# Three parameter loads moved to GpSimd's queue, the weights of gate tiles 0 to 3 issued back to back on SyncE, the parameter transpose moved behind quarter 1, x of block 2 loaded in four parts

## The chip, the cores and the metric

The kernel runs on one core of a Trainium2 chip. Times are device microseconds (us) of one execution; lower is better. A "span" is the time from the first to the last instruction in a trace; the device time of the same execution is 1.7 to 1.9 us longer, and 2.2 to 2.4 us longer in 7 of the 109 executions that have both numbers. A ratio is the mean time of one kernel's runs over that of the other's runs of the same rounds, so it is not quite the ratio of the medians quoted beside it.

Engines: PE is TensorE (matmul), PEld its weight loads, DVE is VectorE, ACT is ScalarE, POOL is GpSimd, SP is SyncE. A name with q, such as SPq, is the engine's instruction stream where it issues DMAs.

## The reference

A layernorm feeds two branches, an S5 state-space scan and a gated MLP, and all is summed. S is 2048, D is 512, F is 1792.

```python
xn = layernorm(x)
# branch A: diagonal complex recurrence
dt = exp(log_dt);  Lam_bar = exp(dt * (Lambda_re + 1j * Lambda_im))
h_t = Lam_bar * h_(t-1) + B_bar @ xn_t
y   = 2 * real(C @ h) + xn * Dskip
# branch B: gated MLP
out_B = (silu(xn @ w1) * (xn @ w3)) @ w2
return x + y + out_B
```

The parameters of this document are the three vectors log_dt, Lambda_re and Lambda_im, 512 bf16 numbers (1 KB) each. They are loaded as 12 rows of 128, transposed on PE, and turned into the table of angles for the scan.

## The kernel before

The start of the kernel issues loads by hand. Everything that SyncE issues goes out in program order:

```python
    def load_w(f0, f1, eng1=nc.sync, eng3=nc.sync):                    # w1: gate side, w3: up side
        eng1.dma_start(out=w1_sb[:, :, f0:f1], in_=w1v[:, :, f0:f1])   # line 151
        eng3.dma_start(out=w3_sb[:, :, f0:f1], in_=w3v[:, :, f0:f1])   # line 152
    ...
    for c in range(2):                                                  # x chunks 0 and 1 in halves
        for eng, dsl in ((nc.sync, slice(0, D // 2)), (nc.scalar, slice(D // 2, D))):
            eng.dma_start(out=x_blk[0][:, c, dsl], in_=xv[:, c, dsl])
    nc.scalar.dma_start(out=x_blk[0][:, 3, :], in_=xv[:, 3, :])
    nc.sync.dma_start(out=x_blk[0][:, 2, :], in_=xv[:, 2, :])
    load_w(0, 2 * P)                                                    # tiles 0 and 1
    for i, src in enumerate((A_log_dt, A_Lambda_re, A_Lambda_im)):      # line 166 is the DMA
        nc.sync.dma_start(out=par_rows[i * NPT:(i + 1) * NPT, :], in_=src.rearrange("(t p) -> t p", p=P))
    load_w(2 * P, 4 * P)                                                # tiles 2 and 3
```

The first block of 512 rows is treated in four quarters of 128 rows, as the x chunks arrive. A quarter's matmuls (line 557) need that chunk normalised and transposed (line 238), and the weights of its tiles. Tiles 0 and 1 write gu_ps, tile 2 writes bu_ps:

```python
            quarter(0, (0, 1), 2)          # needs w1, w3 of tiles 0 and 1
            pps = params_transpose()       # needs par_rows; line 310
            params_dt(pps)
            params_turn()                  # a row of small GpSimd instructions
            table_angles(0)                # VectorE, four instructions each
            table_angles(1)
            quarter(1, (0, 1))
            ln_first_transpose(2)
            quarter(0, (2,))               # needs w1, w3 of tile 2
            ln_first_transpose(3)
            quarter(1, (2,))
            ...                            # [cut: quarters 2 and 3, then 512-column matmuls, line 525]
```

The later loads, issued on SyncE at about 33 us, contain:

```python
        load_x(2)                          # x of block 2, one DMA of 512 KB
        load_x(3)
```

Of the kernel before, what the change touches and what calls it, by code (L numbers as in the profile page):

```python
# [17 lines left out]
P = 128  # L18
# [45 lines left out]
def kernel(  # L64
# [17 lines left out]
    nc = tc.nc  # L82
# [8 lines left out]
    NPT = PS // P  # L91
# [41 lines left out]
    par_rows = const.tile([3 * NPT, P], BF16, name="par_rows")  # L133
# [16 lines left out]
    def load_w(f0, f1, eng1=nc.sync, eng3=nc.sync):  # L150
        eng1.dma_start(out=w1_sb[:, :, f0:f1], in_=w1v[:, :, f0:f1])  # L151
        eng3.dma_start(out=w3_sb[:, :, f0:f1], in_=w3v[:, :, f0:f1])  # L152

    def load_x(b, parts=1):
        n = CPB // parts
        for i in range(0, CPB, n):
            nc.sync.dma_start(out=x_blk[b][:, i:i + n, :], in_=xv[:, b * CPB + i:b * CPB + i + n, :])
# [4 lines left out]
    nc.scalar.dma_start(out=x_blk[0][:, 3, :], in_=xv[:, 3, :])  # L162
    nc.sync.dma_start(out=x_blk[0][:, 2, :], in_=xv[:, 2, :])
    load_w(0, 2 * P)
    for i, src in enumerate((A_log_dt, A_Lambda_re, A_Lambda_im)):
        nc.sync.dma_start(out=par_rows[i * NPT:(i + 1) * NPT, :], in_=src.rearrange("(t p) -> t p", p=P))  # L166
    load_w(2 * P, 4 * P)

    def bulk_loads():
        nc.scalar.activation(out=w1_sb[:, 0, 4 * P:4 * P + 1], in_=rstd_all[:, 0:1], func=ACT.Copy)  # L170
        load_w(4 * P, MID * P)
        load_x(1)
        nc.sync.dma_start_transpose(out=bt[:, 0], in_=A_B_re)
        nc.sync.dma_start_transpose(out=bt[:, 1], in_=A_B_im)
        load_w(MID * P, F)
        nc.sync.dma_start_transpose(out=ct_in[:, :, 0, :], in_=A_C_re)
        nc.sync.dma_start_transpose(out=ct_in[:, :, 1, :], in_=A_C_im)

    def late_loads():
        nc.sync.dma_start(out=w2_sb, in_=B_w2.rearrange("(t p) d -> p t d", p=P))  # L180
        nc.sync.dma_start(out=dskip_row, in_=A_Dskip.partition_broadcast(P))
        load_x(2)
        load_x(3)


# [5 lines left out]
    def keep_busy(n, cols):  # L191
        for _ in range(n):
            nc.tensor.matmul(out=wps[:, 0:cols], lhsT=ones[:, 0:P], rhs=ones[:, 0:cols], start=True, stop=True)
# [4 lines left out]
    nc.gpsimd.memset(ident, 0.0)  # L198
    nc.gpsimd.affine_select(out=ident, in_=ident, compare_op=ALU.not_equal, fill=1.0,
                            base=0, pattern=[[-1, P]], channel_multiplier=1)  # L200
    nc.gpsimd.iota(iota_i, pattern=[[1, TBLK]], base=1, channel_multiplier=0)
    nc.gpsimd.tensor_copy(out=iota_f, in_=iota_i)
    nc.gpsimd.memset(halfpi, float(np.pi / 2))
# [8 lines left out]
    def ln_stats(b, cl):  # L212
        stats = lnp.tile([P, 6], FP32, name="stats", bufs=4)
        nc.vector.bn_stats(out=stats, in_=x_blk[b][:, cl, :])
        nc.vector.bn_aggr(out=mv_all[:, b * CPB + cl, :], in_=stats)
# [10 lines left out]
    def ln_first_rstd(cl):  # L226
        lnv = lnp.tile([P, 1], FP32, name="lnv")
        nc.scalar.activation(out=lnv, in_=mv_all[:, cl, 1:2], func=ACT.Ln, bias=eps_t, scale=1.0)
        nc.scalar.activation(out=rstd_all[:, cl:cl + 1], in_=lnv, func=ACT.Exp, scale=-0.5)

    def ln_first_transpose(cl, parts=1):
        n = NDT // parts
        for i in range(0, NDT, n):
            if parts > 1:
                ln_apply(0, cl, slice(i * P, (i + n) * P))
            pxt = ps_y.tile([P, n, P], BF16, name="y_ps")
            for k in range(n):
                nc.tensor.transpose(out=pxt[:, k, :], in_=xn_blk[0][:, cl, (i + k) * P:(i + k + 1) * P], identity=ident)
            nc.scalar.activation(out=xnT_blk[0][:, i:i + n, cl * P:(cl + 1) * P], in_=pxt, func=ACT.Copy)
# [68 lines left out]
    def params_transpose():  # L308
        pps = ps_y.tile([P, NP3], BF16, name="y_ps")
        nc.tensor.transpose(out=pps, in_=par_rows, identity=ident[0:NP3, 0:NP3])  # L310
        return pps
# [96 lines left out]
    def k_gate(f):  # L408
        return f if f < NFH else NK + f - NFH
# [4 lines left out]
    def act(b):  # L414
        if act_blk[b] is None:
            act_blk[b] = actp.tile([P, 2 * NK, TBLK], FP16, name="act")
        return act_blk[b]
# [101 lines left out]
    def glu(b):  # L519
        xnT = xnT_blk[b]  # L520
        pend = []

        def mms(ps, w, f, tsl):
            for dt in range(NDT):
                nc.tensor.matmul(out=ps[:, tsl], lhsT=w[:, dt, f * P:(f + 1) * P], rhs=xnT[:, dt, tsl],  # L525
                                 start=(dt == 0), stop=(dt == NDT - 1))

        pair = []

        def evac(f, g_ps, u_ps):  # L530
            if f % 2 == 0:
                pair[:] = [glup.tile([P, 2, TBLK], BF16, name="g16"), glup.tile([P, 2, TBLK], BF16, name="u16")]
            g16, u16 = pair
            nc.scalar.activation(out=g16[:, f % 2, :], in_=g_ps, func=ACT.Silu)  # L534
            nc.scalar.activation(out=u16[:, f % 2, :], in_=u_ps, func=ACT.Copy)  # L535
            if f % 2 == 1:
                pend.append((f, g16, u16))

        def gate():
            f, g16, u16 = pend.pop(0)  # L540
            bg.own(0.6, -0.5)
            k0, k1 = k_gate(f - 1), k_gate(f)
            nc.vector.tensor_tensor(out=act(b)[:, k0:k1 + 1:k1 - k0, :], in0=g16, in1=u16, op=ALU.mult)  # L543

        f0 = 0
        if b == 0:
            f0 = FIRST
            tiles = first_ps

            def quarter(cl, fs, parts=1):  # L550
                tsl = slice(cl * P, (cl + 1) * P)
                n = NDT // parts
                for side, w in ((0, w1_sb), (1, w3_sb)):
                    for i in range(0, NDT, n):
                        for f in fs:
                            for dt in range(i, i + n):
                                nc.tensor.matmul(out=tiles[2 * f + side][:, tsl], lhsT=w[:, dt, f * P:(f + 1) * P],  # L557
                                                 rhs=xnT[:, dt, tsl], start=(dt == 0), stop=(dt == NDT - 1))

            ln_stats(0, 0)  # L560
            ln_first_rstd(0)
            bulk_loads()
            ln_stats(0, 1)
            ln_first_rstd(1)
            ln_first_transpose(0, 2)
            keep_busy(4, P)
            ln_apply(0, 1)
            ln_first_transpose(1)
            ln_stats(0, 2)
            ln_first_rstd(2)  # L570
            ln_stats(0, 3)
            ln_first_rstd(3)
            ln_apply(0, 2)
            ln_apply(0, 3)
            quarter(0, (0, 1), 2)
            pps = params_transpose()
            params_dt(pps)
            params_turn()
            table_angles(0)
            table_angles(1)  # L580
            quarter(1, (0, 1))
            ln_first_transpose(2)
            quarter(0, (2,))
            ln_first_transpose(3)
            quarter(1, (2,))
            nc.scalar.activation(out=rho, in_=kr, func=ACT.Exp)
            nc.scalar.preload_act_table_set("silu_and_others")
            quarter(2, range(FIRST))
            for f in range(FIRST):
                quarter(3, (f,))  # L590
            evac(0, tiles[0], tiles[1])
            evac(1, tiles[2], tiles[3])
            evac(2, tiles[4], tiles[5])
            gate()
            bg.tensor(0.0)
            bg.fill()
        for f in range(f0, NFT):
            if f == AHEAD[b]:
                if b == 0:
                    ssm_tasks(0)  # L600
                bu(b)
            g_ps = ps_gu.tile([P, TBLK], FP32, name="gu_ps")
            mms(g_ps, w1_sb, f, slice(0, TBLK))
            u_ps = ps_gu.tile([P, TBLK], FP32, name="gu_ps")
            mms(u_ps, w3_sb, f, slice(0, TBLK))
            evac(f, g_ps, u_ps)
            if b in (1, NBLK - 1) and f == NFT - 3:
                seeds(0 if b == 1 else 4)
            if b == 0 and f == FIRST:
                sin_step((0, 0))  # L610
            elif b > 0 or f != MID - 1:
                sin_step()
            bg.tensor(1.72)
            bg.fill()
            if pend and f % 2 == 0:
                gate()
        return gate
# [182 lines left out]
    for t in ln1b:  # L800
        bg.add(*t, ("ln", 1))
    bg.add(0.0, late_loads, ("ln", 1))
    bg.add(0.2, params_w)
    gate = glu(0)
    bg.flush(("ln", 1))
    gate()
# [92 lines left out]
```

## Time and profile before

| | before |
|---|---|
| device time, first runs | 204.51 us median of 3 (204.32 to 204.8) |
| span of the trace | 203.1 us |
| PE busy | 198.3 us, 98% of the span |
| first 512-column matmul starts | 13.47 us |
| last VectorE instruction ends, to the end of the span | 200.41, 203.06: 2.65 us |

The page of before (busy us, share of the span, instructions):

```profile
span 203.1 us, 3444 instructions
...
PE 198.3 (98%) x1317; PEld 122.8 (60%) x1317; DVE 172.7 (85%) x242; ACT 125.4 (62%) x251; POOL 39.0 (19%) x65
```

The chain of waits of before, in order of time (start us, us, what). Each piece is what the next one waited for; "issue" is the small gap between two instructions:

```profile
2.59 0.51 SPq L152
3.09 0.04 issue
3.14 0.44 SPq L166
3.58 0.05 issue
3.63 0.26 SPq L166
3.89 0.04 issue
3.93 0.29 SPq L166
4.23 0.04 issue
4.27 0.40 SPq L151
4.67 0.04 issue
4.71 5.13 DMA w_sb<-in_B_w_dram
9.85 0.05 issue
9.89 0.40 PE bu_ps L557 x4
...
13.64 8.63 PE gu_ps L525 x40
...
199.31 1.10 DVE xn L735 x4
```

Read it from the bottom up. From 9.89 us on, PE matmuls follow one another almost to the end. The matmul at 9.89 waited for a weight DMA, issued at 4.71, and its issue stood in SyncE's stream behind the three parameter loads (line 166, 3.14 to 4.22).

What PE waited for in the whole run (engine, line, releaser; us in total, times, longest):

```profile
PE bu_ps L557 <- DMA w_sb<-in_B_w_dram: 1.0, 1, 1.0
PE bu_ps L193 <- PEq L883: 0.8, 1, 0.8
```

The second line is the start of the program. So the only wait of PE in this trace is 1.0 us for the up weights of tiles 2 and 3.

### The profile page before, as it was taken

The page shows a single profiled execution, that of the slowest core. Times are in us where ns is not written, and L with a number is a line of the kernel's source. Part 1 is how long each engine was busy: PE and PEld are TensorE (multiplying, and loading weights), DVE is VectorE, ACT ScalarE, POOL GpSimd, SP SyncE. Part 2 cuts the span into 40 slices and gives each one's busy share as a digit, 9 for nine tenths or more (in the row PEclk, how much of TensorE's full clock was granted, in tenths as well). Part 3 has the DMA queues.
Part 4 walks back from the last instruction along what each step waited for, and adds up shares of the span by engine and source line. Part 5 has one row for each costly group of instructions (what it writes and reads, how often), then busy time and mean ns, then how long its engine had stood idle before and what let it go on. Part 6 is the DMA issues. An engine that isn't in the chain of part 4 may idle for free.

```text
span 203.1 us, 3444 instructions
## 1 busy us (share of the span) xinstructions
PE 198.3 (98%) x1317; PEld 122.8 (60%) x1317; DVE 172.7 (85%) x242; ACT 125.4 (62%) x251; POOL 39.0 (19%) x65
## 2 busy tenths in 40 slices
PE   8899999999999999999999999999999999999994
PEld 2784444444444488854444445888444458888993
DVE  3779699999999999989949999999999935584832
ACT  4699897699999977959766676110566662101010
POOL 3250269700310143021111010310101110000000
PEclk9999999999999999999999999999999999999999
DMA  6899999992573042926796004466330780101011
GB/s 173 248 247 191 312 203 106 350 281 42 101 146 66 0 90 57 183 86 118 68 194 131 13 13 94 91 143 132 90 65 0 149 162 2 52 3 52 29 40 39
DMA packets 28696, 23.16 MB, mean 114 GB/s; under 512 B 16008, under 2 KB 26376, under 8 KB 28680
## 3 DMA queue, kind: packets, MB, share of 16 engines
q1 hardware_dynamic: 25512, 13.21, 27.9%
q0 software_dynamic: 2592, 9.44, 24.9%
q10 hardware_dynamic: 576, 0.30, 0.5%
q8 instruction: 10, 0.16, 0.3%
q14 instruction: 6, 0.05, 0.1%
HBM read 7.74 MB, written 2.10 MB: 48 GB/s over the span
## 4 chain that ended last, share of the span: by engine, by line
PE 93%; DMA 3%; SPq 2%; DVE 1%; issue 0%
PE gu_ps L525 45%; PE gu_ps L724 16%; PE y_ps L724 9%; PE bu_ps L724 7%; PE bu_ps L435 7%; PE y_ps L435 7%; DMA w_sb<-in_B_w_dram 3%; PE gu_ps L557 1%; PE bu_ps L557 1%; DVE xn L735 1%; SPq L166 0%; SPq L151 0%; SPq L161 0%; SPq L152 0%; DVE x_blk L735 0%
## 5 line engine op out<-in xcount | busy, mean ns | idle before, releaser
L525 PE MATMUL gu_ps<-xnT,w_sb 128*128 128x512 bf16 x424 | 92.5, 379 | 0.0
L525 PEld LDWEIGHTS <-w_sb 128*128 128x128 bf16 x424 | 41.4, 98 | 49.4
L724 PEld LDWEIGHTS <-act 128*128 128x128 f16 x451 | 43.2, 98 | 5.5
L534 ACT ACTIVATE g<-gu_ps 128x512 bf16<-128x512 f32 x55 | 33.1, 602 | 14.6 <-PE gu_ps L525 14.4
L535 ACT ACTIVATE u<-gu_ps 128x512 bf16<-128x512 f32 x55 | 33.2, 603 | 9.8 <-PE gu_ps L525 9.5
L543 DVE TENSOR_TENSOR act<-g,u 128x1024 f16<-128x1024 bf16 x28 | 19.0, 677 | 4.4 <-ACT u L535 4.4
L435 PEld LDWEIGHTS <-bt 128*128 128x128 bf16 x128 | 12.5, 98 | 15.1
L478 DVE TENSOR_TENSOR_SCAN u<-rho,act,u 128x512 bf16<-128x512 f32 x16 | 19.6, 1266 | 0.0
L492 POOL DMA_DIRECT2D act<-p x8 | 7.2, 900 | 45.8 <-DVE act L488 31.8
L435 PE MATMUL bu_ps<-xnT,bt 128*128 128x512 bf16 x64 | 15.1, 379 | 0.0
L435 PE MATMUL y_ps<-xnT,bt 128*128 128x512 bf16 x64 | 15.1, 379 | 0.0
L457 DVE TENSOR_TENSOR p<-u,tabe 128x2048 bf16<-128x2048 bf16 x8 | 9.8, 1219 | 2.6 <-DMA act<-p 2.5
L724 PE MATMUL y_ps<-tw,act 128*128 128x256 f16 x88 | 10.9, 272 | 0.0
L437 ACT ACTIVATE u<-y_ps 128x512 bf16<-128x512 f32 x16 | 9.5, 595 | 2.3 <-PE y_ps L435 2.1
L724 PE MATMUL gu_ps<-w_sb,act 128*128 128x256 bf16 (+1 forms) x84 | 10.8, 268 | 0.0
L724 PE MATMUL gu_ps<-tw,act 128*128 128x256 f16 x88 | 10.7, 273 | 0.0
L437 ACT ACTIVATE u<-bu_ps 128x512 bf16<-128x512 f32 x16 | 9.5, 595 | 2.0 <-PE bu_ps L435 1.9
L468 POOL DMA_DIRECT2D u<-p x6 | 5.3, 878 | 26.8 <-ACT u L535 7.9
L744 ACT ACTIVATE bu_ps<-y_ps 128x256 f32<-128x256 f32 x4 | 1.5, 369 | 13.7 <-PE y_ps L724 13.7
L461 DVE TENSOR_TENSOR u<-u,tabe 128x2048 bf16<-128x2048 bf16 x8 | 9.8, 1220 | 0.2
L478 DVE TENSOR_TENSOR_SCAN u<-rho,ends,u 128x512 bf16<-128x512 f32 x8 | 9.9, 1268 | 0.0
L484 DVE TENSOR_TENSOR p<-u,tabe 128x2048 f16<-128x2048 bf16 x8 | 9.8, 1221 | 0.1
(143 smaller groups left out, 275.1 us busy)
## 6 DMA issues: line engine op xcount, KB each, us to landing
act<-p POOLq DMA_DIRECT2D x8, 512.0 KB, 4.7
u<-p POOLq DMA_DIRECT2D x6, 512.0 KB, 4.7
xn<-x_blk POOLq DMA_DIRECT2D x4, 512.0 KB, 5.6
out_dram<-xn SPq DMA_DIRECT2D x15, 128.0 KB, 1.7
w_sb<-in_B_w_dram SPq DMA_DIRECT2D x1, 1792.0 KB
x_blk<-in_A_x_dram SPq DMA_DIRECT2D x3, 512.0 KB, 9.0
w_sb<-in_B_w_dram SPq DMA_DIRECT2D x2, 768.0 KB, 7.1
w_sb<-in_B_w_dram SPq DMA_DIRECT2D x4, 256.0 KB, 3.7
```

What stands on the lines that cost most here:

```text
L435: nc.tensor.matmul(out=ps, lhsT=bt[:, ri, dt, pt * P:(pt + 1) * P], rhs=xnT_blk[b][:, dt, :], start=(dt == 0), stop=(dt == NDT - 1))
L437: nc.scalar.activation(out=u[:, j, ri, :], in_=ps, func=ACT.Copy)
L457: nc.vector.tensor_tensor(out=st["p"][:, :, ::-1, :], in0=st["g"], in1=tabe[:, psl, 2:0:-1, :], op=ALU.mult)
L461: nc.vector.tensor_tensor(out=st["g"], in0=st["g"], in1=tabe[:, psl, 0:1, :].to_broadcast(FULL), op=ALU.mult)
L478: nc.vector.tensor_tensor_scan(out=v, data0=rho[:, pt:pt + 1].to_broadcast([P, TBLK]), data1=v, initial=init, op0=ALU.mult, op1=ALU.add)
L484: nc.vector.tensor_tensor(out=st["p16"][:, :, ::-1, :], in0=st["g"], in1=tabe[:, psl, 1:3, :], op=ALU.mult)
L492: gp.dma_start(out=act_state(b, hf), in_=st["p16"], accum_op=ALU.add)
L525: nc.tensor.matmul(out=ps[:, tsl], lhsT=w[:, dt, f * P:(f + 1) * P], rhs=xnT[:, dt, tsl], start=(dt == 0), stop=(dt == NDT - 1))
L534: nc.scalar.activation(out=g16[:, f % 2, :], in_=g_ps, func=ACT.Silu)
L535: nc.scalar.activation(out=u16[:, f % 2, :], in_=u_ps, func=ACT.Copy)
L543: nc.vector.tensor_tensor(out=act(b)[:, k0:k1 + 1:k1 - k0, :], in0=g16, in1=u16, op=ALU.mult)
L724: nc.tensor.matmul(out=out, lhsT=left[:, k, :], rhs=right[k][:, cols], start=(start and k == 0), stop=(k == NK - 1), skip_group_check=True)
```

## The change

The intent: the three small loads leave SyncE's stream, so the weights of tiles 2 and 3 go out 1.13 us earlier; GpSimd, idle at that time, issues the parameters; and since they may arrive later, PE asks for them one quarter later. The third edit, the split of a load at 33 us, comes with it.

```diff
     load_w(0, 2 * P)
-    for i, src in enumerate((A_log_dt, A_Lambda_re, A_Lambda_im)):
-        nc.sync.dma_start(out=par_rows[i * NPT:(i + 1) * NPT, :], in_=src.rearrange("(t p) -> t p", p=P))
     load_w(2 * P, 4 * P)
@@
-        load_x(2)
+        load_x(2, 4)
         load_x(3)
@@
     nc.gpsimd.affine_select(out=ident, ...)
+    for i, src in enumerate((A_log_dt, A_Lambda_re, A_Lambda_im)):
+        nc.gpsimd.dma_start(out=par_rows[i * NPT:(i + 1) * NPT, :], in_=src.rearrange("(t p) -> t p", p=P))
     nc.gpsimd.iota(iota_i, ...)
@@
             quarter(0, (0, 1), 2)
+            quarter(1, (0, 1))
             pps = params_transpose()
             params_dt(pps)
             params_turn()
             table_angles(0)
             table_angles(1)
-            quarter(1, (0, 1))
```

## The prediction

> **What bounds the kernel now.** TensorE. The page gives PE 198.3 of a 203.1 us span (98%), and the chain of waits is an unbroken row of matmuls from 9.89 to 198.87 us. The list of waits for PE holds one real wait in the run: 1.0 us, 8.9 to 9.9, for a weight DMA (up-projection weights of gate tiles 2 and 3). The chain before 9.89 is SyncE's issue row: x, weights of tiles 0-1, three parameter loads (0.44, 0.26, 0.29 us), weights of tiles 2-3, then 5.13 us to the landing at 9.85. The granted clock is 1.0 throughout. So the change can give at most about that 1.0 us.
>
> **What the change does.**
> - It removes three issues from SyncE between 3.14 and 4.27, so both weight loads of tiles 2-3 go out 1.13 us earlier (timeline of SyncE: 4.27 to 3.14, 4.71 to about 3.6). The bulk loads, now at 5.33, go out at about 4.65, when the ScalarE instruction that gates them (4.39 to 4.60) is done: about 0.5 us more distance to the needed loads, so less competition.
> - The windows view shows the DMA engines 0.76 to 1.0 busy from 5.5 to 9 us, with a dip at 5.5 to 6.0 where the second pair of loads arrives late. Not all of 1.13 us will come out at the landing: I estimate 0.5 to 1.1 us, a landing at 8.8 to 9.3.
> - GpSimd gets three issues. Its accumulate DMAs took 0.80 to 0.94 us each, so from 1.32 they should end by about 4.0 us. The Trainium skill ("DMA: Bandwidth & Descriptors", anatomy of one DMA on the GpSimd path) gives about 2.0 us fixed per such DMA: an estimated landing near 6 us; PE asks at about 8.4. Iota and cast (0.56 and 0.61 us) slip to 4.0 to 5.3, first needed after 9 us.
> - The parameter transpose (0.18 us of PE) moves behind quarter 1 (1.07 us). The first angle table on VectorE moves from 9.11 to about 9.7, the eight table instructions end near 13.9 instead of 13.4. The gate after them now waits 1.29 us for ScalarE (14.66) and could start near 13.8: about even, so VectorE, almost never idle from 15 to 75 us, moves forward about 0.7 us.
> - The x load of block 2 in four parts adds three issues (estimated 0.45 us each) at 35 us on SyncE; nothing on PE waits there.
>
> The same page says that several issuing engines save only issue time ("Issuing engines are not separate DMA queues"). That issue time is what is on the chain here.
>
> **Sum.** PE's wait of 1.0 us falls to 0 to 0.5; nothing is added to PE. Gain about 0.8 us: **203.7 us, 8 in 10 between 203.2 and 204.5**. Faster by over 2%: 0.01; within 2%: 0.98; slower: 0.01.
>
> **What would show it.** Right: weights of tiles 2-3 issued at 3.1 and 3.6; PE's wait before its first bu_ps matmul on weights 0 to 0.5 us; the row of matmuls unbroken from about 9.0; parameter transpose at 8.3 to 8.5 without a wait. Wrong: PE waiting for par_rows; the landing still near 9.8; VectorE's first normalisation (4.73) or statistics stretched by GpSimd's work; a new PE wait later.
>
> **What would make it wrong.** GpSimd's DMA landing after 8.4; one lagging DMA engine deciding the landing whatever the issue time; early PE time taken back later by VectorE.

## The result, and the profile after

| | before | after |
|---|---|---|
| device time, median | 204.43 us (204.32 to 204.8, 4 runs) | 203.87 us (203.79 to 204.41, 4 runs) |
| ratio of the runs | | 0.9975, 95% interval 0.9954 to 0.9997 |
| span of the trace | 203.1 us | 202.6 us |
| first 512-column matmul starts | 13.47 us | 13.01 us |
| last VectorE instruction to the end | 2.65 us | 2.65 us |

The traced execution of the changed kernel is the slowest of its four (204.41). The other three have spans of 202.0 to 202.1 us.

The page of after:

```profile
span 202.6 us, 3438 instructions
...
PE 197.4 (97%) x1304; PEld 122.5 (60%) x1317; DVE 172.5 (85%) x242; ACT 125.1 (62%) x251; POOL 44.2 (22%) x68
```

PE's 13 missing instructions are matmul records lost from the trace, since the weight loads are all there. The timeline of SyncE after (start us, us, engine, line, operation, what):

```profile
2.11 0.43 SPq L151 DMA_DIRECT2D w_sb<-in_B_w_dram  x1
2.59 0.51 SPq L152 DMA_DIRECT2D w_sb<-in_B_w_dram  x1
3.14 0.51 SPq L151 DMA_DIRECT2D w_sb<-in_B_w_dram  x1
3.69 0.51 SPq L152 DMA_DIRECT2D w_sb<-in_B_w_dram  x1
4.85 0.37 SPq L151 DMA_DIRECT2D w_sb<-in_B_w_dram  x1
```

and of GpSimd:

```profile
1.50 0.74 POOL L200 DMA_DIRECT2D par_rows<-in_A_log_dt_dram  x1 [0.18 <-issue]
2.23 0.56 POOL L200 DMA_DIRECT2D par_rows<-in_A_Lambda_re_dram  x1
2.78 0.50 POOL L200 DMA_DIRECT2D par_rows<-in_A_Lambda_im_dram  x1
```

The four weight loads now go out at 2.11, 2.59, 3.14 and 3.69. The chain of waits after:

```profile
2.59 4.79 DMA w_sb<-in_B_w_dram
7.38 0.04 issue
7.42 1.51 PE gu_ps L557 x24
8.93 0.11 PE y_ps L310
9.04 0.33 PE y_ps L238 x4
9.37 0.45 PE bu_ps L557 x8
...
13.44 8.37 PE gu_ps L525 x38
...
198.85 1.09 DVE xn L735 x4
```

And PE's waits after:

```profile
PE bu_ps L191 <- PEq L883: 0.8, 1, 0.8
PE gu_ps L557 <- DMA w_sb<-in_B_w_dram: 0.6, 1, 0.6
```

The wait of 1.0 us for the second pair of weights (bu_ps) is gone, and there is one of 0.6 us for the up weights of the first pair (gu_ps), which were issued at 2.59 in both kernels and landed about 0.9 us later than before. Parameters and second pair were there in time: the transpose (L310) and tile 2 (bu_ps) follow without a wait. So the trace shows about half of the gain (0.46 us at the first 512-column matmul), and a new question: why did a load that was not touched arrive later?

The semaphore records of the traces tell more of both waits. A load reports its end in 16 arrivals and has landed with the last. In before, 15 arrivals of the second pair's up weights had come by 8.58 us, and the last came at 9.85; PE was free for them at 8.88. In after, 15 arrivals of the first pair's up weights had come by 6.72 us and the last at 7.38; PE was free at 6.85. So in both first traces PE waited for one late part out of 16.

### The profile page after: what moved, and what is told of

Same layout as the page of the kernel before. It is cut to its first block, busy times and chain, and to the rows that moved or that the text cites. A ratio compares the mean times of both kernels' runs of the same rounds, so it can differ in the third digit from the quotient of the medians.

```text
span 202.6 us, 3438 instructions
## 1 busy us (share of the span) xinstructions
PE 197.4 (97%) x1304; PEld 122.5 (60%) x1317; DVE 172.5 (85%) x242; ACT 125.1 (62%) x251; POOL 44.2 (22%) x68
## 4 chain that ended last, share of the span: by engine, by line
PE 94%; DMA 2%; SPq 1%; DVE 1%; issue 1%
PE gu_ps L525 45%; PE gu_ps L724 16%; PE y_ps L724 9%; PE bu_ps L724 7%; PE y_ps L435 7%; PE bu_ps L435 7%; DMA w_sb<-in_B_w_dram 2%; PE gu_ps L557 2%; PE bu_ps L557 1%; DVE xn L735 1%; SPq L161 0%; PE y_ps L238 0%; SPq L151 0%; DVE x_blk L735 0%; SPq L163 0%
```

## The experiments

The landings quoted are the start of the issue plus the view's issue-to-landing time, which is rounded to 0.1 us.

### The changed kernel twice more

No edit. The first of the two runs:

> The changed kernel unchanged, for a second trace and a tight interval. Theory A (the weights of tiles 2 and 3, sent 1.13 us earlier, end PE's 1.0 us wait; the 0.57 us wait for the up weights of tiles 0 and 1 in the first trace is a matter of that execution, since it was the slowest of four, 202.6 against 202.0 to 202.1 us): ratio 0.996 to 0.998; if this trace is one of about 202.0 us, it shows the up weights of tiles 0 and 1 at 6.8 us or earlier and no wait over 0.2 us on weights. Rival B (the earlier second pair always pushes the first pair's landing back, 6.5 to about 7.4): the same wait of 0.4 us or more stands here too, whatever the span.

Measured: 203.97 us median (203.8 to 204.09, 6 runs) against 204.3 us, ratio 0.9979 (0.9961 to 0.9997). In this trace, of span 201.8 us, the up weights of tiles 0 and 1 landed at 6.6 us and PE waited for no DMA (15 arrivals by 6.49, the last at 6.59). So neither the wait nor its absence is the rule.

The second:

> The changed kernel, unchanged, for a third trace and for comparison on the chip of the next two. Theory V: 203.8 to 204.2 us, ratio 0.997 to 0.999; PE never waits for tiles 2 and 3 (they land by 9.1 us), and waits 0 to 0.6 us for the up weights of tiles 0 and 1, whose landing varies from 6.6 to 7.4 us. Rival: another wait, or none, with a span of over 202.3 us.

Measured: 204.19 us median (203.77 to 204.61) against 204.34 us, ratio 0.9984 (0.9959 to 1.001). This trace (202.4 us) has the wait again, 0.6 us, with the up weights of tiles 0 and 1 landing at 7.2 us; the second pair's landed at 9.0. (PE's wait list also has 0.5 us for xn here, but the first transpose of xn started at 5.01 us, as early as elsewhere.)

### The kernel before once more

No edit.

> The kernel before, unchanged, for a second trace. Theory V (the 1.0 us wait of the first trace is one draw: the landing of the up weights of tiles 2 and 3 varies, since two traces of variants that leave the issue order alone had it at 8.6 and 9.0 us, with PE waiting 0.1 and 0.3 us): ratio 0.998 to 1.002, spans of the executions spread by 1 us or more, and this trace's wait tells its span (about 201.9 us plus the wait, within 0.25 us). Rival (the wait is always near 1.0 us): 0.8 to 1.1 us in this trace too, and spans within 0.4 us.

Measured: 204.19 us median against 204.34 us for the shared runs of the same kernel, ratio 0.999 (0.9963 to 1.0018); spans from 201.9 to 203.1 us. PE's waits in this trace:

```profile
PE bu_ps L193 <- PEq L883: 0.8, 1, 0.8
PE y_ps L310 <- DMA par_rows<-in_A_Lambda_im_dram: 0.7, 1, 0.7
PE bu_ps L557 <- DMA w_sb<-in_B_w_dram: 0.3, 1, 0.3
```

The sum is 1.0 us again, but 0.7 of it is a wait of the parameter transpose for the last parameter row, which the first trace did not have. Theory V holds in that the time is a draw, the spans spread by 1.2 us, and 201.9 plus the waits gives this trace's span of 202.8. The rival's number for the sum came true in this trace, from another wait.

### The transpose's place alone

Before, with the second diff of the `quarter` block only (the three parameter loads stay on SyncE).

> The kernel before with only the parameter transpose moved behind quarter 1. Theory A: no gain, 204.3 to 204.6 us, ratio 0.999 to 1.001, PE still waits about 1.0 us for the weights of tiles 2 and 3 at 8.9 us, and the angle tables start 0.5 to 1 us later. Rival D (part of the gain is the order of PE's work): ratio 0.998 or lower.

Measured: 204.3 us median against 204.3, ratio 0.9997 (0.9976 to 1.0019). Theory A is right about the time. It is wrong about the trace: in this execution the up weights of tiles 2 and 3 landed at 9.0 us, and PE lost only about 0.3 us to weights (span 202.2). SyncE also issued that load only at 5.22 us here, after a wait of 0.5 us for an x load, and yet it landed earlier than in the first trace of before, where it was issued at 4.71.

### The queue alone, and the queue with the transpose

The first kernel is the changed one with two of its edits taken back, the second with only the split taken back:

```diff
 # queue_only: both hunks; queue_and_transpose: the first hunk alone
-        load_x(2, 4)
+        load_x(2)
@@
             quarter(0, (0, 1), 2)
-            quarter(1, (0, 1))
             pps = params_transpose()
             ...
             table_angles(1)
+            quarter(1, (0, 1))
```

> Parameters on GpSimd's queue and weights back to back, but the parameter transpose still ahead of quarter 1 and x of block 2 in one load. Theory A (only the issue order matters): the same as the changed kernel within 0.15 us, since in its trace the parameters landed at about 7.0 us and PE would ask at about 7.3 or later. Rival C (the move of the transpose is needed because the parameters land late on GpSimd's queue): slower than the changed kernel by 0.3 us or more, with PE waiting for par_rows.

Measured: 205.22 us median (204.9 to 205.69), ratio 1.0044 (1.0024 to 1.0065): 1.25 us slower than the changed kernel (203.97). That is rival C's number, but not its reason: PE did not wait for par_rows at all. The first 512-column matmul started at 12.32 us, 1.15 us earlier than in the first trace of before, and the span was 203.1 us all the same. PE's row was as rigid as ever; the time was lost after it. From the last VectorE instruction (ending at 199.26) to the end took 3.81 us instead of 2.65 in before.

The DMA views of 198 to 202.6 us show it, first for before:

```profile
q1 hardware_dynamic: 288, 0.16, 11.7%
q10 hardware_dynamic: 144, 0.03, 3.1%
...
out_dram<-xn SPq DMA_DIRECT2D x1, 32.0 KB, 1.5
out_dram<-xn ACTq DMA_DIRECT2D x1, 32.0 KB, 1.7
```

and for the variant with the queue alone:

```profile
q1 hardware_dynamic: 288, 0.16, 11.7%
q10 hardware_dynamic: 144, 0.03, 3.3%
q14 instruction: 1, 0.01, 0.9%
...
out_dram<-xn ACTq DMA_DIRECT2D x1, 32.0 KB, 2.4
out_dram<-xn SPq DMA_DIRECT2D x1, 32.0 KB, 2.2
```

The lines with q1, q10 and q14 are queues (packets, MB, share of the engines' time); the last two are the last two stores of the output, with KB and us from issue to landing. One packet is new (433 against 432): an instruction fetch (q14), of 8192 bytes at 200.28 us in the trace's packet records, in the middle of the last stores. In before the fetch of that kind lies at 194.3 us. The two stores took 2.4 and 2.2 us to land instead of 1.7 and 1.5, and in the semaphore records 15 of the 16 arrivals of each are early and one comes 0.6 to 0.9 us after them, which points to one late DMA engine. SyncE also lost time between its last two stores. The lines of the timeline, first before, then the queue alone:

```profile
200.00 0.81 SPq L738 DMA_DIRECT2D out_dram<-xn  x2
198.85 1.19 SPq L738 DMA_DIRECT2D out_dram<-xn  x2
```

Its last store started at 199.71, 0.53 us after the end of the one before it, where before has 0.10 us between the same two.

The theory formed here (F): SyncE's instructions are fetched in blocks, and where in the program a block ends depends on how many instructions SyncE has. Three loads fewer push the fetch by two stores, into the tail. The split of x of block 2 into four adds exactly three loads.

> The changed kernel without its third edit: x of block 2 again in one load, so SyncE issues three DMAs fewer than in both kernels. Theory F (found in the trace of the variant with the queue change alone: SyncE's next block of instructions is fetched by an 8 KB transfer at 200.3 us, among the last stores, instead of at 193 to 194 us; the split only puts back the three instructions that left): row of matmuls from about 9 us as in the changed kernel, but 3.7 to 4.0 us from the last VectorE instruction to the end instead of 2.6, and 0.9 to 1.4 us slower than the changed kernel (ratio to before 1.002 to 1.006). Rival (the split is of no weight, and the transpose's place was what the queue-only variant lacked): as the changed kernel, ratio 0.996 to 0.999.

Measured: 205.29 us median (204.99 to 205.99), ratio 1.0042 (1.002 to 1.0063). Fetch at 200.9 us, 3.81 us from the last VectorE instruction to the end, and again 2.4 and 2.2 us for the last two stores. The transpose's place changes nothing of it.

### The queue with the split, transpose ahead of quarter 1

The changed kernel with only the second hunk above.

> The changed kernel with the parameter transpose left ahead of quarter 1. Theory F: as fast as the changed kernel, ratio 0.996 to 0.999, tail 2.6 us, fetch at 193 to 194 us, PE does not wait for par_rows by more than 0.2 us. Rival (the transpose's move is needed): 0.5 us or more slower than the changed kernel.

Measured: 204.22 us median (203.7 to 204.73), ratio 0.9985 (0.9963 to 1.0007); 2.65 us at the end, fetch at 193.5 us, no wait of PE for par_rows. With the parameters on GpSimd's queue, the last of them landed at 6.8 us and PE asked at 7.65. The place of the transpose has no effect that these runs could tell from nothing. The late start of this trace (first 512-column matmul at 12.68 us) came from x and not from weights: ScalarE's half of x chunk 1 landed at 4.3 us (3.3 to 4.0 in the other traces), and the first transpose of xn started at 5.52 us (4.96 to 5.23 in the others).

### The split alone

Before, with `load_x(2)` made `load_x(2, 4)`.

> The kernel before with only x of block 2 in four loads: three DMAs more on SyncE. Theory F: the fetch comes three DMAs earlier than before's 194.3 us and disturbs nothing; the only cost is the rotation of the eight DMA semaphores, which puts the last one three places earlier in SyncE's final row of waits (0.3 us in the trace of the variant with parameters last on SyncE): ratio 1.000 to 1.002. Rival (splitting x helps by itself): ratio 0.998 or lower.

Measured: 204.18 us median against 204.61, ratio 0.9985 (0.9965 to 1.0005): unclear, between the two theories. The trace has the 2.93 us at the end that theory F gave (fetch at 191.6 us), but the execution was one in which the second weight pair landed at 8.6 us, so the span is 202.1. By its time alone, the split without the rest cannot be told from the changed kernel (0.9975, 0.9979, 0.9984). What speaks against it as the source of the gain is the trace, where it only lengthens the end, and the two kernels without the split: taking the 1.16 us that their end is longer from their times leaves an estimated 0.3 us of gain in each.

### Eight loads more

Is it the fetch, or is it the order of the DMA semaphores? The DMAs of SyncE and ScalarE take turns over eight semaphores, and at the end SyncE waits for the eight in a fixed order, about 0.06 us each. Three loads fewer also shift which of them the last stores use. Eight loads more leave that order as it is, and move the fetch:

```diff
-        nc.sync.dma_start(out=w2_sb, in_=B_w2.rearrange("(t p) d -> p t d", p=P))
+        w2v = B_w2.rearrange("(t p) d -> p t d", p=P)
+        for t0, t1 in ((0, 5), (5, 10), (10, NFT)):
+            nc.sync.dma_start(out=w2_sb[:, t0:t1, :], in_=w2v[:, t0:t1, :])
@@
         load_x(2, 4)
-        load_x(3)
+        load_x(3, 4)
```

> The changed kernel with x of block 3 in four loads too and w2 in three: eight SyncE DMAs more than in the variant without the split, so the semaphores of the last stores rotate to the same places as there, while the instruction fetch moves eight DMAs. Theory F (the fetch among the last stores is the cost): no fetch after 195 us, tail 2.6 to 2.9 us, within 0.4 us of the changed kernel. Rival S (the rotation of the semaphores is the cost): a tail of 3.7 us or more and 0.9 us or more slower than the changed kernel, as without the split.

Measured: 204.39 us median (203.89 to 204.81), ratio 0.9994 (0.9969 to 1.0018). Fetch at 185.3 us, 2.85 us at the end, and the last stores take 1.6 and 1.7 us. The DMA view of 198 to 202.6 us:

```profile
q1 hardware_dynamic: 288, 0.16, 11.8%
q10 hardware_dynamic: 144, 0.03, 3.1%
...
out_dram<-xn SPq DMA_DIRECT2D x1, 32.0 KB, 1.6
out_dram<-xn ACTq DMA_DIRECT2D x1, 32.0 KB, 1.7
```

Rival S falls: the same semaphores with the fetch elsewhere cost 0.2 us of tail, not 1.2. Nine of the fourteen traces side by side:

| kernel | SyncE loads against before | first 512-column matmul | span | difference | last VectorE instruction to end | last 8192-byte fetch before the end |
|---|---|---|---|---|---|---|
| before | 0 | 13.47 | 203.06 | 189.59 | 2.65 | 194.3 |
| before, again | 0 | 13.29 | 202.85 | 189.56 | 2.64 | 194.1 |
| after | 0 | 13.01 | 202.59 | 189.58 | 2.65 | 193.8 |
| after, again | 0 | 12.23 | 201.81 | 189.58 | 2.64 | 193.1 |
| queue and split | 0 | 12.68 | 202.26 | 189.58 | 2.65 | 193.5 |
| split alone | +3 | 12.25 | 202.12 | 189.87 | 2.93 | 191.6 |
| eight more | +5 | 12.73 | 202.66 | 189.93 | 2.85 | 185.3 |
| queue alone | -3 | 12.32 | 203.07 | 190.75 | 3.81 | 200.3 |
| queue and transpose | -3 | 12.90 | 203.64 | 190.74 | 3.81 | 200.9 |

The column "difference" is the point: from the first 512-column matmul to the end, the kernel takes 189.6 us whatever happened earlier, plus what its last stores cost. Only the start and the tail vary. The other five traces fit: 189.93 for the parameters last on SyncE (+3 loads, fetch at 192.4), 189.57 to 189.59 for the other four (0 or +1 load, fetch at 193.4 to 193.8).

The 0.4 us that SyncE loses goes with the fetch too. SyncE stood still for 0.44 to 0.46 us after one of its stores at 184.10 (eight more), 190.48 (split alone), 191.27 (parameters last), 192.43 (weights before x2 and x3, below), 199.18 (queue alone) and 199.76 us (queue and transpose), and the fetch started 1.1 to 1.2 us after the end of that store each time. Only in the last two was the next store due just then; in the traces with as many loads as before, the same place lies in a long wait for VectorE, where it would not show.

### Parameters last on SyncE's queue

The changed kernel with the three loads on SyncE behind the four weight loads, nothing on GpSimd's queue.

> The changed kernel, but with the parameters on SyncE's queue behind the weights of tiles 2 and 3 (issued at about 4.2 to 5.2 us), nothing on GpSimd's queue. Theory A (issue order of the weights is all): the weights land as in the changed kernel; the parameters land at about 8.5 to 9.5 us, so PE may wait for them up to 0.7 us at 8.4; time equal to the changed kernel or up to 0.7 us slower. Rival E (GpSimd's small packets, at 3.1 to 6.3 us, delay the first weights): the up weights of tiles 0 and 1 land by 6.6 us here, and where the parameters are there in time the kernel is faster than the changed one by 0.2 us or more.

Measured: 205.14 us median (204.76 to 205.65), ratio 1.0036 (1.0016 to 1.0057): slower by 1.17 us than the changed kernel, more than either theory allowed. The trace is of the fastest of its six executions (span 202.9). In it the up weights of tiles 0 and 1 landed at 7.2 us, with no packet of GpSimd's in the way, and PE waited 0.4 us for them. So rival E falls as it was stated: a landing as late as this needs no packets of GpSimd's. It does not need earlier bulk loads either, which went out at 5.43 us here and at 5.33 in before. What this trace shares with those of the changed kernel is that the second pair follows the first at once; how that delays the first pair is not shown. The tail was 2.95 us (three DMAs more than before). What the slower five executions lost was not traced and stays open; the parameters, issued last, are the natural suspect.

### The first weights ahead of x chunks

An attempt at a better version: get the first weight pair ahead of the crowd. The first kernel moves SyncE's x chunk 2 behind it, the second also ScalarE's x chunk 3:

```diff
 # weights_before_x2_x3; weights_before_x2 leaves chunk 3 on nc.scalar where it was
-    nc.scalar.dma_start(out=x_blk[0][:, 3, :], in_=xv[:, 3, :])
-    nc.sync.dma_start(out=x_blk[0][:, 2, :], in_=xv[:, 2, :])
     load_w(0, 2 * P)
+    for c in (2, 3):
+        nc.sync.dma_start(out=x_blk[0][:, c, :], in_=xv[:, c, :])
```

> The changed kernel with SyncE's load of the third x chunk (128 KB) behind the first two weight loads instead of ahead of them. Theory W (with the four weight loads back to back, the first pair's up weights land at about 7.1 us because the engines' queues are full; whatever stands ahead of them counts): they land 0.3 to 0.5 us earlier, at most 6.8 us, PE's wait for them goes to 0 to 0.2 us, median 0.1 to 0.4 us under the changed kernel's of this call, while the third chunk's statistics move by at most 0.3 us. Rival X (the x chunks are then late and the normalisation of the third chunk holds PE up): no gain, or up to 0.3 us slower, with PE or its weight load waiting for xn at about 8.3 us.

Measured: 204.49 us median (204.31 to 204.59), ratio 1.0001 (0.9976 to 1.0027); the changed kernel had 204.19. The up weights of tiles 0 and 1 landed at 6.6 us and PE did not wait for them, as theory W said. But x chunk 2 landed at 6.9 us, and PE's waits are:

```profile
PE y_ps L238 <- DVE xn L219: 0.8, 2, 0.6
PE bu_ps L191 <- PEq L883: 0.8, 1, 0.8
```

0.6 us of the first line is the third chunk's transpose, waiting for its normalisation, as rival X said.

> The same, with the fourth x chunk too moved from ScalarE's queue to SyncE's behind the first weight pair (both x chunks land later, at an estimated 6.0 to 6.6 us). Theory W: up weights of tiles 0 and 1 land at 6.4 us or earlier, no PE wait on them; but the statistics of chunks 3 and 4 start about 0.5 to 1 us later, so the gain over the variant before is 0.1 us or less, or a loss of up to 0.5 us. Rival X: 0.3 to 0.8 us slower than the changed kernel, with PE waiting for xn.

Measured: 204.6 us median (204.15 to 205.36), ratio 1.001 (0.9983 to 1.0037). The up weights landed at 5.9 us, PE waited for xn again (0.7 us in two waits), and the median is 0.4 us above the changed kernel's. In these two traces, both orders trade a wait for weights for a wait for x. No version that was run beats the changed kernel.

## Why the prediction was right or wrong

**The bound and the direction were right.** PE's row is rigid (189.6 us from the first 512-column matmul in every trace with the same tail), so only what happens before about 13 us and after the row can change the time. The measured 203.87 us lies in the range, close to the predicted 203.7. Part of that is luck: the range, 203.2 to 204.5, would have held no change at all (204.43), and the split, which the prediction took to be harmless, is what kept the time from about 205.3 us (the kernel with the other two edits alone), outside the range.

**The gain was half of what was predicted: the mis-sized term is "PE's wait of 1.0 us falls to 0 to 0.5", gain about 0.8.** The three comparisons of the two kernels give ratios of 0.9975, 0.9979 and 0.9984, which is 0.5, 0.4 and 0.3 us; the third interval alone reaches past 1. Two things were off.

- *The 1.0 us was one draw*, taken from an execution slower than the four timed beside it (204.89 us), and made by one late part of 16. The prediction had named this among what would make it wrong (one lagging DMA engine); it did not allow for it in the sum. Traces with before's issue order had the up weights of tiles 2 and 3 at 9.8, 9.7, 9.0 and 8.6 us. Of 43 executions of before, the fastest took 203.73 us, as fast as the changed kernel's fastest of 16 (203.77). Against 203.73, before lost 0.7 us on average (mean 204.42) and the changed kernel 0.3 us (mean 204.03); the runs of before are from four calls, those of the changed kernel from three of them. In these executions the change does not lower the floor; it cuts the slow executions, which reach 205.13 before and 204.61 after.
- *Part of it came back as a wait that was not foreseen.* The landing of the second pair was predicted at 8.8 to 9.3 us and came at 8.4 to 9.1. But a load issued 1.13 us earlier landed only about 0.5 us earlier (median of the traces 9.3 and 8.8), and the first pair paid for it: its up weights moved from 6.5 to 6.7 us (four traces) to 6.6 to 7.4 us (the eight traces with the four weight loads back to back). PE waits for these instead, 0 to 0.6 us. Without the last of the 16 arrivals the move is from 6.3 to 6.5 us to 6.5 to 7.0 us (medians 6.4 and 6.6); in four of the eight traces the last arrival comes another 0.5 to 0.7 us later, which stays unexplained. The Trainium skill says, in "DMA: Bandwidth & Descriptors", section "Issuing engines are not separate DMA queues", that moving issues elsewhere saves only the issue time. These traces agree: 1.13 us of issue time was saved, and the median landing gained no more than that, 0.5 us. In them the loads ahead of the moved ones also landed later.

**GpSimd's loads: right in effect, wrong in the numbers.** The issues took 0.74, 0.56 and 0.50 us, less than estimated from the large accumulate DMAs, and from issue to landing they took 3.3 to 4.2 us in the first trace. The estimate with the skill's fixed 2.0 us ("DMA: Bandwidth & Descriptors", "Anatomy of one DMA — SWDGE (gpsimd) path") gave 6 us; the last row landed at about 7.0, before PE asked at 8.87. GpSimd's work did not stretch VectorE's first statistics, which took 0.69 us in both first traces. One reading of the prediction was off: in half-microsecond windows the DMA engines are 0.65 to 0.98 busy from 5.5 to 9 us in before, not 0.76 to 1.0.

**The transpose's move: no effect that was measured.** It is worth nothing alone (0.9997), and with the parameters on GpSimd's queue the kernel without it is within the noise (0.9985 against 0.9979 and 0.9984). The second trace of before, where PE waited 0.7 us for the parameters, shows the wait that it guards against; the earlier issue on GpSimd removed that wait in all traces.

**VectorE's move was a draw too.** In the first trace the first angle table started at 10.31 us, not 9.7, and the first gate product at 14.51 against 14.66: a gain of 0.15 us and not 0.7. But the gate product started at 13.70 and 14.32 us in the other two traces of the changed kernel, and at 14.46 in the second of before. No wait of PE came of it.

**The split of x was misjudged.** The prediction said that it adds three issues and that nothing on PE waits there. That is true, and misses what it does. Without the split, the kernel is slower than before by 0.4% (1.0042 and 1.0044), because SyncE's instruction fetch falls among the last stores. This is shown by the two kernels without the split, by the one that restores the split alone (queue and split, 0.9985), and by the eight further loads. That SyncE's loss of 0.4 us goes with the fetch is shown by the six traces in which both move together; what SyncE does in it is not. The longer tail of the variant with the queue alone adds up from 0.4 us of late issue, 0.5 us of late landing, and 0.2 us of waits still to be run through behind it; these last come with the order of the semaphores (2.85 us with the fetch elsewhere), so about 1.0 us is left for the fetch.

**Open:** why one part of a load comes up to 1.3 us after the other 15 in some executions, how much of the 0.4 us of mean gain each change of the start brings (in the traces the first 512-column matmul starts at 12.91 us on average in the four with before's order and at 12.71 in the eight with the new one, too few to tell), and the time of the slower executions of the variant with the parameters last on SyncE.

## What to carry to other kernels

A wait in one trace is one draw: before costing a change on it, take a second trace of the kernel before, and compare the spread of the executions, since the fastest ones may not have the wait at all. Here the loads ahead of the moved ones landed later, so look at what the loads ahead of the moved one will do, and not only at the moved one. When a change removes or adds instructions on an engine that issues the last stores, compare the time from the last compute instruction to the end, and look there for an instruction fetch that was elsewhere before; here three loads more moved it away.

## What the Trainium skill lacked or had wrong

- "Runtime: NRT & Kernel Launch", section "Instruction fetch mechanics", gives the cost of crossing a block of instructions as "one DMA tail-bump, mostly hidden", and blocks of 16 KiB. Here it cost about 1.0 us when it fell among the last stores (a tail of 3.81 us against 2.85 with the same order of semaphores), and the packets that moved with SyncE's instruction count were of 8192 bytes, while others in the trace were of 16384.
- No page has a figure for what a fetch costs the data transfers of the same time: the last two stores, with 32 KB each, took 2.4 and 2.2 us to land instead of 1.7 and 1.5, each held up by one of its 16 semaphore arrivals.
- "DMA: Bandwidth & Descriptors", "Anatomy of one DMA — SWDGE (gpsimd) path", gives a fixed cost of about 2.0 us per DMA, and no figure for such a DMA beside other loads. Loads of 1 KB took 3.3 to 4.2 us from issue to landing in the first trace of the changed kernel, beside SyncE's and ScalarE's loads.
- The same page says that issuing engines share the DMA engines, but has no figure for how a following load delays one ahead of it: 1.13 us earlier issue of the second pair gave about 0.5 us earlier landing (medians), and the first pair's second load landed up to 0.9 us later. Nor has it a figure for how far one of the 16 parts of a load can fall behind the other 15: 1.3 us here (9.85 and 8.58 us).
- No page says that the place of the last DMA's semaphore in the final row of waits costs time: 0.2 to 0.3 us (2.85 and 2.93 against 2.65 us), at about 0.06 us per wait left.
